# First layer's first pair of steps nested as well, the layer's pools opened after attention's are closed

## The chip, the cores and the metric

The kernel runs on one core of one Trainium2 chip. The metric is the device time of one execution in microseconds (us), taken as the median over runs. The engines are PE (TensorE, matrix products), DVE (VectorE), ACT (ScalarE), POOL (GpSimd) and SP (SyncE, which here only issues transfers). Each runs its own list of instructions in order and waits for the others on semaphores.

## The reference

Hashed attention, then a feed-forward layer. The results are float32; the two weight matrices come as float64.

```python
mask = q_bucket[:, :, :, None] == k_bucket[:, :, None, :]     # buckets: signs of q @ proj, k @ proj
scores = np.where(mask, q @ k.T / sqrt(D), -1e9)              # B, H, S, D = 4, 8, 768, 64
x = (softmax(scores) @ v)  -> (3072, 512)
h = x @ w_in                                                  # (512, 2048)
g = h * (1.0 / (1.0 + np.exp(-1.702 * h)))
out = g @ w_out                                               # (2048, 512)
```

## The kernel before

**Attention** (`attention`, to about 309 us) works through 16 pairs of heads. Its results stay transposed in `xT` (512 features by 3072 tokens). A pair's results are divided by their softmax sums at the end of the pair by `invert` and `norm` (L575 to L590, on DVE); for the last pair this runs when PE has already begun with the layer. The weights `w_in` arrive as float64 and are converted on the way (`convert`, L170 to L208: one transfer, six DVE steps, one square on ACT). The last two of their 16 chunks are left over (`LATE`) for the layer.

**The first product of the layer** (`feed_forward`) is `xT` by `w_in`, in three blocks of 1024 tokens (`sb`) and eight steps (`mt`) in a block, 24 in all. A step multiplies a 2 by 2 block matrix by another with seven products instead of eight (`product`, i = 1 to 7, L901), each two 128 by 128 weights against 512 tokens. For this it needs sums of quarters of the weights (`in_sums`, on POOL, L222 to L225, kept in `s_in` and, one of them, in `w_in_sb`) and of the tokens (`x_sums`, on DVE, L232 and L233, kept in `t_x`). After the products, ACT copies and DVE adds (L919) form four results u, v, c21, c22, ACT applies the activation (L916) and a transfer keeps them in `g_dram`. POOL then forms four sums of the four results for the second product (`g_outer`, L230 to L233) and SP stores these.

**Nested steps.** Steps are taken two at a time as a pair `t` where `t` lies in `NESTED`. Then three of the seven products (2, 4 and 3, for u, c21 and v) are split once more in the same way (`nested`): seven half-width products of 256 tokens (L971) take the place of four of 512. They need sums of their own: of the weights (`nest_w`, L222 to L225 on 128x128, kept in `nest`) and of the tokens (`nest_x`, L957 to L960, kept in rooms of `w_out_sb`). The other four products (1, 6, 5, 7) stay whole: `p1(0), p1(1), p6(0), p5(0), p6(1), p5(1), p7(0), p7(1)`. `plan(t, at, f)` puts a piece of work behind the `at`-th of these eight, and `play` issues it there; the numbers above 8 fall into the next pair. So the order on every engine is written out by hand by these plans.

**Buffers.** The four results of a pair lie in the pool `stage` for even `t` and in `twice` for odd `t`, so pair t + 2 writes where pair t was. Its first copy `u` (L1025) must wait until POOL has formed the sums that read pair t's `u` and SP has stored them. PSUM holds the accumulating banks: two of kind "a" (products 1, 6, 7), one of kind "b" (product 5), one "c" and the pool `inner` for the nested ones. Because "b" is one bank, `p5(1)` waits until DVE has added and ACT has copied `p5(0)` (L1035).

**Before the change** pair 0 isn't nested: its steps 0 and 1 run as `hidden(0, 0)` and `hidden(0, 1)`, each with seven whole products and a choice of eight banks. The first is built inside `attention`, after the pool that holds the exponentials is closed and while attention's other pools are still open: `attention` ends with `early.close()`, `whole(inverse)`, `norm(last)`, `next(ff)`. A one-element POOL copy, `behind_sums` (L1314), waits for the token sums ahead of `in_sums(1)` and `in_sums(2, 2)`. The pools `twice`, `nest`, `wop` (w_out and the rooms of `nest_x`) and `cv` open after `hidden(0, 0)`, and pairs 1 to 10 are nested.

**The second product** (L1240, from 585 us) multiplies what `g_dram` holds by `w_out`; its code isn't touched.

A part of the code behind a branch (`shifted_attention` and a second `feed_forward`) is not executed on these inputs.

Of the kernel before, what the change touches and what calls it, by code (L numbers as in the profile page):

```python
# [38 lines left out]
def kernel(  # L39
# [254 lines left out]
    def attention(ff):  # L294
# [4 lines left out]
        with actx:  # L299
# [463 lines left out]
            early.close()  # L763
            whole(inverse)
            norm(last)
            next(ff)


    def shifted_attention():
# [76 lines left out]
    def feed_forward(tag, late=()):  # L846
# [9 lines left out]
        with ExitStack() as fctx:  # L856
# [2 lines left out]
            late = list(late)  # L859

            outer = fctx.enter_context(tc.tile_pool(name=f"f0{tag}", bufs=1, space=PSUM, side="right"))
            small_ctx = fctx.enter_context(ExitStack())
            inner = None
            twice_ctx = fctx.enter_context(ExitStack())
            twice = None
            nest_ctx = fctx.enter_context(ExitStack())
            nest = None
            MT = FC // 2
            NESTED = range(1, MT + 3)
            sets = [small_ctx.enter_context(tc.tile_pool(name=f"f1{tag}", bufs=1, space=PSUM, side="right"))]  # L870
            todo, turn = {}, [-1]

            def outer_bank(name):
# [11 lines left out]
            def staged_pair(name, second):  # L885

                held[name] = (twice if second else stage).tile([P, 2 * XT], F32, tag=name, name=name)
                return held[name]

            def staged(name, n):  # L890

                if n in (0, 2 * NESTED.stop) and (name, n) not in made:
                    made[name, n] = staged_pair(name, n > 0)
                return held[name][:, n % 2 * XT : (n % 2 + 1) * XT]

            made = {}
# [115 lines left out]
            def pair_of_steps(t):  # L1012

                sb, m0 = divmod(2 * t, MT)
                tiles, a = {}, [None, None]

                def place(name, i):
                    if name not in tiles:
                        tiles[name] = staged_pair(name, t % 2 == 1)
                    return tiles[name][:, i * XT : (i + 1) * XT]  # L1020

                def p1(i):
                    a[i] = outer_bank("a")
                    product(a[i], sb, m0 + i, 1)
                    nc.scalar.copy(place("u", i), a[i])  # L1025

                def p6(i):
                    product(a[i], sb, m0 + i, 6, False)
                    nc.scalar.copy(place("v", i), a[i])

                def p5(i):
                    b = outer_bank("b")
                    product(b, sb, m0 + i, 5)
                    add(place("v", i), b, place("v", i))
                    nc.scalar.copy(place("c22", i), b)  # L1035

                def p7(i):
                    product(a[i], sb, m0 + i, 7, False)
                    add(place("c22", i), a[i], place("c22", i))
                    nc.scalar.copy(place("c21", i), a[i])  # L1040
                    if i:
                        emit(tiles["c22"])
                        keep(sb, m0, 3, tiles["c22"], nc.scalar)

                def done(at):
                    def f(x):
                        emit(x)
                        if at is not None:
                            keep(sb, m0, at, x, nc.scalar)
                    return f  # L1050

                def small(tag):
                    return lambda: inner.tile([P, XT], F32, tag=tag, name="small")

                for o, name, first, bank_of, at in ((2, "u", 3, lambda: outer_bank("c"), 0),
                                                    (3, "v", 4, small("y"), None), (4, "c21", 9, small("z"), 2)):
                    for i, f in zip((0, 2, 4, 6, 7), nested(o, sb, t, tiles, name, bank_of, done(at))):
                        plan(t, first + i, f, small=True)

                def g_part(i, j):  # L1060
                    x = [tiles[x].rearrange("p (m t) -> p m t", t=XT) for x in ("u", "v", "c21", "c22")]
                    if len(spare[t].shape) == 4 and i == 3:
                        x = [y.rearrange("p m (k t) -> p m k t", k=spare[t].shape[2]) for y in x]
                    g_outer(sb, m0, *x, x[0], x[3], spare[t])[i][j]()


                for i, at in enumerate((12, 13, 14, 17)):
                    for j in range(2):
                        plan(t, at + j, lambda i=i, j=j: g_part(i, j))
                order = (p1, 0), (p1, 1), (p6, 0), (p5, 0), (p6, 1), (p5, 1), (p7, 0), (p7, 1)  # L1070
                for at, (f, i) in enumerate(order, 1):
                    f(i)
                    play(8 * t + at)
# [222 lines left out]
            def conversions(cv, psum, chunks):  # L1296


                gens = [convert(cv, *x, nc.scalar if i else None, psum) for i, x in enumerate(chunks)]
                dma = next(gens[0])  # L1300
                if late:

                    behind_issue(dma, stored[2])
                yield
                for i, x in enumerate(gens):
                    for at in range(6):
                        next(x, None)
                        if at == 3 and i + 1 < len(gens):
                            next(gens[i + 1])
                        yield  # L1310


            behind_sums = stage.tile([1, 1], F32, name="behind_sums", bufs=1)
            nc.gpsimd.tensor_copy(behind_sums, t_x[0:1, 2, 0, 0:1])  # L1314
            for f in in_sums(1) + in_sums(2, 2):
                f()
            hidden(0, 0)
            yield
            twice = twice_ctx.enter_context(tc.tile_pool(name=f"tw{tag}", bufs=1, side="right"))
            nest = nest_ctx.enter_context(tc.tile_pool(name=f"ne{tag}", bufs=1, side="right"))  # L1320
            wop = fctx.enter_context(tc.tile_pool(name=f"wo{tag}", bufs=1))
# [27 lines left out]
            places += [[xT[:, k, XT * j : XT * (j + 1)] for k in (1, 0) for j in range(2)] + places[0][4:],  # L1349
                       [xT[:, k, XT * j : XT * (j + 1)] for k, j in ((2, 1), (0, 3), (1, 3), (1, 1), (0, 1), (2, 3))]]  # L1350
            places = [[x[:, j * TH : (j + 1) * TH] for x in y for j in range(2)] for y in places]
            more, w_sums = nest_x(0, places[0]), nest_w(1)
            x = todo.pop(1, [])
            hidden(0, 1, more[2] + w_sums[2] + more[3] + w_sums[3] + x[:4], x[4:])
            yield
            small_ctx.close()
            inner_ctx = fctx.enter_context(ExitStack())
            inner = inner_ctx.enter_context(tc.tile_pool(name=f"in{tag}", bufs=1, space=PSUM, side="right"))
            plan(1, 1, *more[4], *w_sums[4])
            for t in NESTED:  # L1360
                sb, at = divmod(t, MT // 2)
                if at == 0:
                    for i, f in enumerate(more[2] + more[3]):
                        plan(t, 1 + i // 2, f)
                    plan(t, 8, *(x[3] for x in x_sums))
# [169 lines left out]
```

## Time and profile before

| | |
|---|---|
| three runs | 847.32, 847.37, 848.08 us; median 847.37 |
| the profiled execution | 847.66 us |
| its span, first to last instruction | 845.9 us |
| granted TensorE clock | 0.997 |
| DVE busy | 674.9 us (80%) |
| ACT busy | 337.6 us (40%) |
| POOL busy | 382.3 us (45%) |
| moved by DMA | 144.92 MB |

How to read the profile: times are us from the start of the span unless ns is written. A row of the timeline gives start, duration, engine, source line, operation, output <- input, shapes, how many instructions were merged, and in brackets the idle time ahead of it with what ended it. A row of the chain gives start, duration, what. Each float32 matmul shows as two instructions, so a whole product (two weights) shows as x4 and a nested one as x2. Ends of matmuls are modelled, and merged rows of PE overlap the next by 0.16 us.

### The profile page before, as it was taken

How to read it: one execution, taken by the hardware profiler on the slowest of the kernel's cores; microseconds unless marked ns; L12 is line 12 of the kernel's file. 1: busy time of each engine (PE TensorE's matmuls, PEld its weight loads, DVE VectorE, ACT ScalarE, POOL GpSimd, SP SyncE). 2: the span in 40 equal slices, each digit the busy share in tenths (PEclk: the TensorE clock that was granted, in tenths of full speed). 3: DMA queues.
4: the chain of work that ended last, by engine and by line, in shares of the span. 5: the costliest groups of instructions: out<-in, count | busy, mean ns of one | idle time of the engine just before them, and what ended most of it. 6: DMA issues, size and time to landing. Idle time of an engine off the chain costs nothing.

```text
span 845.9 us, 14969 instructions
## 1 busy us (share of the span) xinstructions
PE 835.8 (99%) x5662; PEld 522.2 (62%) x5662; DVE 674.9 (80%) x1073; ACT 337.6 (40%) x550; POOL 382.3 (45%) x324
## 2 busy tenths in 40 slices
PE   8999999999999999999999999999999999999996
PEld 4444444444444444556666666656888888888885
DVE  5478888887888985786878678858999987797776
ACT  6766766766676634444444444443000000000000
POOL 4433443343334359999844686858865100000000
PEclk9999999999999999999999999999999999999998
DMA  9688666677674104446555546667844486467524
GB/s 142 121 156 172 152 137 142 139 153 148 152 160 100 50 2 174 149 139 235 205 195 200 221 174 224 221 226 249 303 182 165 177 236 256 155 194 249 199 100 101
DMA packets 165341, 144.92 MB, mean 171 GB/s; under 512 B 124112, under 2 KB 140112, under 8 KB 160272
## 3 DMA queue, kind: packets, MB, share of 16 engines
q1 hardware_dynamic: 154352, 110.54, 46.9%
q10 hardware_dynamic: 10912, 33.39, 11.8%
q8 instruction: 45, 0.74, 0.4%
q14 instruction: 32, 0.26, 0.1%
HBM read 79.69 MB, written 50.33 MB: 154 GB/s over the span
## 4 chain that ended last, share of the span: by engine, by line
PE 98%; DMA 1%; DVE 0%; SPq 0%; issue 0%; DVEq 0%
PE product L1240 30%; PE product L901 22%; PE s L547 15%; PE s L514 15%; PE small L971 7%; PE product L971 4%; PE s L496 2%; PE s L460 1%; PE s L569 1%; DMA pj<-in_proj_dram 1%; PE s L410 0%; DVE feat L411 0%; DVE own L405 0%; DVE y L1220 0%; SPq L385 0%
## 5 line engine op out<-in xcount | busy, mean ns | idle before, releaser
L484 ACT ACTIVATE e<-s 128x768 f32<-128x768 f32 x192 | 143.2, 811 | 48.5 <-PE s L514 43.9
L547 PE MATMUL s<-e,v 128*32 128x385 f32 x1536 | 130.9, 488 | 0.0
L525 POOL TENSOR_TENSOR t_x<-e 128x768 f32<-128x768 f32 x32 | 60.5, 1892 | 136.7 <-ACT e L484 131.8
L901 PE MATMUL product<-xT,w_in_sb 128*128 128x512 f32 x208 | 96.8, 592 | 0.0
L547 PEld LDWEIGHTS s<-e,v 128*32 128x32 f32 x1536 | 46.7, 109 | 79.3 <-issue 62.2
L901 PE MATMUL product<-t_x,s_in 128*128 128x512 f32 x192 | 89.7, 592 | 0.0
L514 PE MATMUL s<-s_in 32*128 32x384 f32 x912 | 87.8, 481 | 0.0
L525 POOL TENSOR_TENSOR t_x<-t_x,e 128x768 f32<-128x768 f32 x32 | 55.2, 1725 | 43.4 <-ACT e L484 42.0
L538 DVE TENSOR_TENSOR acc<-acc,e 128x768 f32<-128x768 f32 x63 | 70.1, 1112 | 2.3
L1276 ACT COPY wide<-product 128x256 f32<-128x256 f32 x20 | 7.4, 371 | 157.7 <-PE product L1240 116.2
L901 PEld LDWEIGHTS product<-xT,w_in_sb 128*128 128x128 f32 x208 | 39.4, 190 | 31.8 <-issue 28.9
L514 PEld LDWEIGHTS s<-s_in 32*128 32x128 f32 x912 | 43.9, 185 | 23.4 <-issue 2.2
L901 PEld LDWEIGHTS product<-t_x,s_in 128*128 128x128 f32 x192 | 36.4, 190 | 28.1 <-issue 25.6
L919 DVE TENSOR_TENSOR u<-product,u 128x256 f32<-128x256 f32 (+1 forms) x64 | 29.7, 478 | 23.5 <-PE product L971 21.2
L514 PE MATMUL s<-own 32*128 32x384 f32 x432 | 44.2, 482 | 0.0
L465 DVE TENSOR_SCALAR f<-s,above,weight 128x384 bf16<-128x384 f32 x15 | 10.2, 677 | 39.6 <-PE s L569 28.9
L230 POOL TENSOR_TENSOR u<-v,u 128x1024 f32<-128x1024 f32 (+1 forms) x12 | 26.2, 2184 | 20.8 <-ACT v L916 12.4
L919 DVE TENSOR_TENSOR c<-small,c 128x256 f32<-128x256 f32 (+1 forms) x60 | 26.8, 461 | 9.8 <-PE small L971 9.5
L535 DVE SCALAR_TENSOR_TENSOR acc<-t_x,e 128x768 f32<-128x768 f32 x31 | 29.3, 945 | 6.1 <-POOL t_x L525 3.5
L919 DVE TENSOR_TENSOR v<-small,v 128x256 f32<-128x256 f32 (+1 forms) x60 | 27.1, 465 | 8.4 <-PE small L971 5.8
L1035 ACT COPY c<-product 128x512 f32<-128x512 f32 x20 | 11.7, 586 | 52.2 <-DVE v L919 46.7
L1240 PE MATMUL product<-s_in,xT 128*128 128x256 f32 x136 | 31.3, 379 | 0.0
(302 smaller groups left out, 1808.0 us busy)
## 6 DMA issues: line engine op xcount, KB each, us to landing
raw_g<-g_dram SPq DMA_DIRECT2D x20, 1024.0 KB, 6.1
s_in<-g_dram SPq DMA_DIRECT2D x18, 1024.0 KB, 5.9
g_dram<-c ACTq DMA_DIRECT2D x20, 512.0 KB, 3.1
raw<-in_moe_w_out_dram ACTq DMA_DIRECT2D x16, 512.0 KB, 3.8
raw<-in_moe_w_in_dram ACTq DMA_DIRECT2D x15, 512.0 KB, 3.8
s_in<-own SPq DMA_DIRECT2D x36, 192.0 KB, 4.0
v<-in_v_dram SPq DMA_DIRECT2D x16, 384.0 KB, 4.2
g_dram<-u ACTq DMA_DIRECT2D x10, 512.0 KB, 2.9
```

What stands on the lines that cost most here:

```text
L230: return [lambda: eng.tensor_tensor(t1, b12, b11, op=Alu.subtract), lambda: eng.tensor_tensor(b12, b22, b12, op=Alu.subtract), lambda: eng ...
L484: nc.scalar.activation(es[c][:, kt, :, 0:HS], ps[:, :, 0:HS], Act.Exp, scale=1.0 / D**0.5)
L496: nc.tensor.matmul(ps[:, j, 0:HS], a[hs, keys], m[hs, cols], start=at == 0, stop=at == 1)
L514: nc.tensor.matmul(ps[i][:, j, 0:HS], a[r0 : r0 + 32, keys], m[r0 : r0 + 32, cols], start=at == 0, stop=at == 2)
L525: nc.gpsimd.tensor_tensor(low_sum, low_sum if i else e[:, 0], e[:, i + 1], op=Alu.add)
L535: nc.vector.scalar_tensor_tensor(acc, terms[0], T * TINY, terms[1], op0=Alu.add, op1=Alu.add)
L538: nc.vector.tensor_tensor(acc, acc, terms[i + 1], op=Alu.add)
L547: nc.tensor.matmul(av[D * j + d : D * j + d + 32, :], vt[:, j, row, d : d + 32], es[c][:, t, j, :], start=(t == 0), stop=(t == T - 1))
L901: nc.tensor.matmul(ps, wq[LEFT[i]][:, kc, :], xq[RIGHT[i]][:, kc, :], start=(start and kc == 0), stop=(kc == K2 - 1), skip_group_check=not ...
L919: nc.vector.tensor_tensor(dst, x, y, op=Alu.add)
L971: nc.tensor.matmul(x, wq[LEFT[i]], xq[RIGHT[i]], start=start, stop=True, skip_group_check=True)
L1240: nc.tensor.matmul(ps, wq[LEFT[i]][:, c, :], gq[RIGHT[i]][:, c, :], start=(onto is None and c == 0), stop=(c == F4 - 1), skip_group_check= ...
```

## The change

- `NESTED` begins at 0: pair 0 is nested like the others, and `hidden(0, 0)`, `hidden(0, 1)`, `behind_sums` and the small PSUM pool for them go.
- `next(ff)` at the end of `attention` goes: the layer's first pools open after all of attention's are closed.
- POOL's sums for pair 0 (`in_sums(1)`, and those of `nest_w(0)` and `nest_x(0)`) are put in the order in which its products use them; those of pair 1 and `in_sums(2, 2)` follow. `nest_w(0)` is no longer formed a second time at pair 3.
- In pair 0 the nested products stand later: u behind products 4, 6, 7, 9, 10, v behind 6, 7, 8, 10, 11 (otherwise 3, 5, 7, 9, 10 and 4, 6, 8, 10, 11).
- The transfer for the first late chunk of `w_in` is no longer put behind a store, and its conversion falls into pair 0.

```diff
@@ attention
             whole(inverse)
             norm(last)
-            next(ff)
@@ feed_forward
-            small_ctx = fctx.enter_context(ExitStack())
-            NESTED = range(1, MT + 3)
-            sets = [small_ctx.enter_context(tc.tile_pool(name=f"f1{tag}", bufs=1, space=PSUM, side="right"))]
+            NESTED = range(MT + 3)
+            sets = []
...
-                for o, name, first, bank_of, at in ((2, "u", 3, lambda: outer_bank("c"), 0),
-                                                    (3, "v", 4, small("y"), None), (4, "c21", 9, small("z"), 2)):
-                    for i, f in zip((0, 2, 4, 6, 7), nested(o, sb, t, tiles, name, bank_of, done(at))):
-                        plan(t, first + i, f, small=True)
+                for o, name, by, bank_of, at in ((2, "u", (3, 5, 7, 9, 10) if t else (4, 6, 7, 9, 10), lambda: outer_bank("c"), 0),
+                                                 (3, "v", (4, 6, 8, 10, 11) if t else (6, 7, 8, 10, 11), small("y"), None),
+                                                 (4, "c21", (9, 11, 13, 15, 16), small("z"), 2)):
+                    for i, f in zip(by, nested(o, sb, t, tiles, name, bank_of, done(at))):
+                        plan(t, i, f, small=True)
...
-                dma = next(gens[0])
-                if late:
-
-                    behind_issue(dma, stored[2])
+                next(gens[0])
...
-            behind_sums = stage.tile([1, 1], F32, name="behind_sums", bufs=1)
-            nc.gpsimd.tensor_copy(behind_sums, t_x[0:1, 2, 0, 0:1])
-            for f in in_sums(1) + in_sums(2, 2):
-                f()
-            hidden(0, 0)
-            yield
...
-            more, w_sums = nest_x(0, places[0]), nest_w(1)
-            x = todo.pop(1, [])
-            hidden(0, 1, more[2] + w_sums[2] + more[3] + w_sums[3] + x[:4], x[4:])
-            yield
-            small_ctx.close()
             inner_ctx = fctx.enter_context(ExitStack())
             inner = inner_ctx.enter_context(tc.tile_pool(name=f"in{tag}", bufs=1, space=PSUM, side="right"))
-            plan(1, 1, *more[4], *w_sums[4])
+
+            more, w_sums = nest_x(0, places[0]), nest_w(0)
+            for f in in_sums(1) + w_sums[2][:3] + more[2][:3]:
+                f()
+            plan(0, 2, *w_sums[3][:3], *more[3][:2], *w_sums[2][3:], *more[2][3:], *more[3][2:], *w_sums[3][3:])
+            plan(0, 7, *w_sums[4], *more[4])
             for t in NESTED:
                 sb, at = divmod(t, MT // 2)
-                if at == 0:
+                if at == 0 and t:
...
-                if t + 1 <= MT // 2:
-                    w_sums = nest_w((t + 1) % (MT // 2))
-                    if t + 1 < MT // 2:
-                        plan(t, 4 if t == 1 else 1, *in_sums(2 * t + 2, 2))
-                    plan(t, 6 if t == 1 else 3, *w_sums[2], *w_sums[4], *w_sums[3])
+                if t + 1 < MT // 2:
+                    w_sums = nest_w(t + 1)
+                    plan(t, (5, 4, 1)[t], *in_sums(2 * t + 2, 2))
+                    if t:
+                        plan(t, 6 if t == 1 else 3, *w_sums[2], *w_sums[4], *w_sums[3])
+                    else:
+                        plan(1, 1, *w_sums[2], *w_sums[3])
+                        plan(1, 5, *w_sums[4])
```

More of the change, by code (lines that the diff above doesn't have):

```diff
@@ L890, in staged @@
             def staged(name, n):
-                if n in (0, 2 * NESTED.stop) and (name, n) not in made:
-                    made[name, n] = staged_pair(name, n > 0)
+                if n == 2 * NESTED.stop and (name, n) not in made:
+                    made[name, n] = staged_pair(name, True)
                 return held[name][:, n % 2 * XT : (n % 2 + 1) * XT]
```

## The prediction

> **What bounds the kernel now.** I read the page first, for the engines and the chain that ended last, and then the table by stages for the first four pairs of steps.
>
> ```profile
> span 845.9 us, 14969 instructions
> PE 835.8 (99%) x5662; PEld 522.2 (62%) x5662; DVE 674.9 (80%) x1073; ACT 337.6 (40%) x550; POOL 382.3 (45%) x324
> ...
> PE 98%; DMA 1%; DVE 0%; SPq 0%; issue 0%; DVEq 0%
> ```
>
> ```profile
> 308.89:332.97 24.08, 24.08 (x58) 10.69 (x58) 15.98 (x24) 9.59 (x16) 20.83 (x23) 1.00 0.34 121
> 332.97:350.17 17.20, 17.20 (x50) 9.13 (x49) 13.06 (x22) 6.34 (x11) 16.42 (x24) 1.00 0.40 138
> 350.17:372.96 22.79, 22.79 (x76) 14.05 (x75) 18.58 (x35) 8.85 (x13) 21.69 (x34) 1.00 0.28 93
> ```
>
> The columns of the second view are length, busy time of PE, weight loads, DVE, ACT and POOL, then clock and DMA. PE is the chain, and in these stages (steps 0 and 1, pair 1, pair 2) it is busy for the whole length. So before the change no wait costs anything here, and the change can gain only by giving PE less to do. The same rows show what stands behind PE: POOL is busy for 21.69 of 22.79 us. PE is full, and POOL almost.
>
> **Less work for PE.** The durations of a product are those of the chain:
>
> ```profile
> 340.81 1.72 PE product L901 x4
> 342.53 0.86 PE product L971 x4
> ```
>
> A whole product (x4) takes 1.72 us; the second row holds two nested ones, 0.43 us each. Steps 0 and 1 are 14 whole products, 14 x 1.72 = 24.08, the length of the first stage. Nested, pair 0 is 8 whole and 21 nested ones: 13.76 + 9.03 = 22.79. The change takes **1.29 us** from PE, no more. The Trainium skill (Perfetto Trace Analysis, Matmuls) says that larger matmuls are more efficient than smaller ones; here half the width takes exactly half the time, so the measurement decides, and if the rule ate the whole gain the result would be 1.3 us higher.
>
> **The first wait: product 5 of step 1.** The start of the layer lies beside the end of attention on DVE:
>
> ```profile
> 311.62 1.56 DVE L233 TENSOR_TENSOR t_x<-xT,t_x 128x1024 f32<-128x1024 f32 x1
> 313.11 0.94 DVE L590 TENSOR_TENSOR xT<-xT,rs 128x768 f32<-128x768 f32 x1
> ...
> 318.15 1.29 DVE L590 TENSOR_TENSOR xT<-xT,rs 128x768 f32<-128x768 f32 x1
> ...
> 340.49 0.69 DVE L919 TENSOR_TENSOR v<-product,v 128x512 f32<-128x512 f32 x1
> ```
>
> ```profile
> 341.22 0.59 ACT L1035 COPY c<-product 128x512 f32<-128x512 f32 x1 [1.79 <-DVE v L919]
> ```
>
> DVE is at attention's sums without a pause until its last `norm` (L590) ends at 318.15 + 1.29 = 319.44. Before, `hidden` had eight banks and nothing on PE needed DVE until then. Now pair 0 has one bank "b": p5(1) must wait until DVE has added p5(0) (L919, 0.69) and ACT has copied it (L1035, 0.59), and the add is queued behind that `norm`. PE comes to p5(1) after p1, p1, p6, p5 (6.88), one nested product (0.43) and p6 (1.72): 308.89 + 9.03 = 317.9.
>
> When does the `norm` end? POOL and DVE hold each other up where both run sums out of SBUF:
>
> ```profile
> 310.52 1.59 POOL L225 TENSOR_TENSOR s_in<-w_in_sb,s_in 128x256 f32<-128x256 f32 x1
> 313.39 0.70 POOL L1314 COPY behind_sums<-t_x 1x1 f32<-1x1 f32 x1 [1.29 <-DVE t_x L233]
> ...
> 316.67 0.73 POOL L225 TENSOR_TENSOR s_in<-w_in_sb,s_in 128x256 f32<-128x256 f32 x1
> ...
> 318.71 1.87 POOL L223 TENSOR_TENSOR w_in_sb<-w_in_sb 128x512 f32<-128x512 f32 x1
> ```
>
> The same sum takes POOL 1.59 us beside DVE's L232 and L233 and 0.73 us beside a transpose; the last `norm` takes 1.29 us beside POOL's L223 and the one before it 0.94. After the change POOL is idle at the last `norm` (0.35 less), but the four sums of `in_sums(1)` move forward from behind `behind_sums` to 312.1, against L233, the earlier `norm` and L208. Bounds: 319.1, if they cost DVE nothing more than before, and 320.2, if DVE waits out one and a half of them besides (0.73 each). I take 319.6, nearest to the row of before. The Trainium skill (SBUF — State Buffer, Who interferes with whom) says that a DVE instruction with two SBUF inputs and a POOL instruction that reads SBUF exclude each other for the whole instruction; the rows agree in size, and by the full rule for two of DVE's sums I would put it at 319.8, 0.2 us more in the result.
>
> So p5(1) starts at 319.6 + 0.69 + 0.59 and about 0.1 for the two hand-overs, at 320.95: **PE waits 3.0 us** where it waited for nothing.
>
> **POOL starts late.** In the built program POOL's first sum for pair 0's nested weights (`w20`) waits for that same last `norm`, since `nest` now lies where attention's pools lay. The row of `behind_sums` shows such a release: DVE ended at 311.62 + 1.56 = 313.18, POOL began at 313.39. So POOL stands idle from about 315.2, when `in_sums(1)` is done, to 319.8, and everything for pairs 0 to 3 queues behind that. The durations, as distances between starts:
>
> ```profile
> 329.51 0.73 POOL L957 TENSOR_TENSOR w_out_sb<-xT 128x256 f32<-128x256 f32 x1
> ...
> 332.39 0.46 POOL L222 TENSOR_TENSOR w<-w_in_sb 128x128 f32<-128x128 f32 x1
> 332.93 0.45 POOL L223 TENSOR_TENSOR w_in_sb<-w_in_sb 128x128 f32<-128x128 f32 x1
> 333.34 0.46 POOL L224 TENSOR_TENSOR w<-w,w_in_sb 128x128 f32<-128x128 f32 x1
> ...
> 334.30 0.73 POOL L957 TENSOR_TENSOR w_out_sb<-xT 128x256 f32<-128x256 f32 x1
> ...
> 349.10 1.28 POOL L222 TENSOR_TENSOR s_in<-w_in_sb 128x512 f32<-128x512 f32 x1
> 354.28 0.46 POOL L222 TENSOR_TENSOR w<-w_in_sb 128x128 f32<-128x128 f32 x1
> 365.15 0.46 POOL L222 TENSOR_TENSOR w<-w_in_sb 128x128 f32<-128x128 f32 x1
> ```
>
> (The last three rows begin groups with others between.) Four `nest_x` sums take 332.39 - 329.51 = 2.88, four `nest_w` sums 1.91, `in_sums` of two steps 354.28 - 349.10 = 5.18. Nested product 6 of u needs the fifth POOL sum, 319.8 + 2.95 = 322.75; PE is there at 320.95 + 1.72 = 322.67. Each such meeting (u's, v's and then c21's product 6, whose sums stand behind `in_sums(2, 2)`) costs between 0 and 0.4; I take **0.6 us** in all. To this point PE is 3.0 + 0.6 - 1.29 = 2.3 us later than before.
>
> **The wait that decides: pair 3 takes over pair 1's buffers.**
>
> ```profile
> 370.49 2.36 POOL L230 TENSOR_TENSOR u<-v,u 128x1024 f32<-128x1024 f32 x1
> 372.93 2.37 POOL L231 TENSOR_TENSOR v<-c,v 128x1024 f32<-128x1024 f32 x1
> 375.37 2.36 POOL L232 TENSOR_TENSOR c<-c,u 128x1024 f32<-128x1024 f32 x1
> ...
> 380.14 0.46 POOL L222 TENSOR_TENSOR w<-w_in_sb 128x128 f32<-128x128 f32 x1
> ```
>
> ```profile
> 378.18 1.07 ACT L1025 COPY u<-product 128x512 f32<-128x512 f32 x2 [2.04 <-DMA g_dram<-u]
> ```
>
> ```profile
> 378.93 1.88 PE L901 MATMUL product<-t_x,s_in 128*128 128x512 f32 x4
> ```
>
> Pair 3's copy of u (ACT, two of 0.59 merged) waits until POOL's L232 has read pair 1's u and SP has stored it; it begins 2.81 us after L232. Pair 3's p6(0) overwrites the bank that it reads, and starts at 378.93; the first copy is done at 378.77. Before the change this fitted with 0.16 us to spare. Afterwards POOL's list from 319.8 to that L232 is: weights and tokens of u and v 2 x 1.91 + 2 x 2.88 = 9.58; `in_sums(2, 2)` 5.18; c21's 1.91 + 2.88; pair 1's u and v weights 3.82; L230 of pair 0 2.44; `in_sums(4, 2)` 5.18; c21's weights 1.91; L231, L232 of pair 0 4.88; pair 2's weights 5.73; L233 2.44; `in_sums(6, 2)` 5.18; pair 3's weights 370.49 - 365.15 = 5.34; L230, L231 of pair 1 4.88. Sum 61.35. A sum that needs the one right before it starts 0.54 after it, otherwise 0.41 (332.39, 332.93, 333.34); the new order has about five fewer such neighbours, so 60.75. L232 begins at 319.8 + 60.75 = 380.55 instead of 375.37, **5.2 us later**; less the spare time (0.16, of which 0.05 is the hand-over) PE's p6(0) is 5.1 us later than before, at 384.0. By its own work and the first waits it would be there at 381.2, so this wait takes in the 2.3 us and is not added to it. Bounds of the list: 60.0, if every sum runs without the 0.13, and 61.9.
>
> **Nothing later gives back or adds.** Before, POOL formed `nest_w(0)` again at 380.14, 5.7 us of work, which is gone now; so POOL is 0.5 us ahead for pair 2's sums while PE is 5.1 later. The first late chunk of `w_in` starts to load at the `norm` and has some 5 us until DVE comes to it; pair 0's stores go by ACT (0.33 each) beside idle time of ACT. If such cover failed, it would cost under 1 us and end inside the 2.8 us that PE waits at pair 3.
>
> The sum: 847.66 (profiled execution; 845.9 of span and 1.76 around it) + 5.1 = 852.8. The median of the runs is 0.29 below the profiled one, so **852.5**.
>
> **Rivals.** (a) *Only the first waits count* (8%): POOL gets through its list 2.8 us faster than its rows say, and +2.3 remains: 849.7. Against it: from 329.51 to 375.37 POOL's rows of before follow each other without idle time. (b) *Not slower* (5%): the last `norm` doesn't hold the layer, PE keeps its 1.29 us, 846.1. Place: the release of POOL's `w20` and of DVE's first add. It decides only if both come by 316.5 for p5(1), and POOL's list by 313.3 for pair 3 (375.37 - 1.3 - 60.75); DVE's rows stand against it, for it only that the two engines would disturb each other less. That nested products don't do what they say (no gain on PE) is 1.3 above any of these, but the rows of pairs 1 and 2 speak against it. (c) *More than one takeover waits* (8%): stores of v and c22 of pair 1, which also come after POOL's later sums, hold pair 3's copies long enough to stop p5(1) too, another 2 to 3 us, 855. Against: ACT needs that copy only some 9 us after p6(0). The forecast has the other 79%.
>
> **Numbers.** For the forecast: `norm` 319.1 to 320.2 and list 60.0 to 61.9 give +3.9 to +6.8, as ends that won't all meet; 850.9 to 854.2 takes most of it, and leaves (a), (b) and (c) out. About 0.2% (1.7 us) is what a measurement of this kernel can tell from no change. Even the ideal, 1.29 us, is within that: faster 1%, same 5%, slower 94%.
>
> **What would show it.** In the profile after: PE's rows with about 3 us of nothing before the second p5 near 318 to 321; POOL idle from about 315 to 320, released by DVE's L590; POOL's second L230 group (pair 1's) about 5 us later than 370.49; a gap of about 2.8 us on PE before pair 3's p6(0), with ACT's u copy released by POOL or the store; and no gap from there on. I am wrong if POOL's first nested sum starts before the last `norm`, or if the gap at pair 3 isn't there.

## The result and the profile after

After: **851.83 us** median of six runs (851.45 to 853.37); before, beside it: 847.35 us (six runs, 846.68 to 848.08). The ratio is 1.0057 (95% interval 1.0044 to 1.0070), some 4.5 us slower. The profiled execution of after took 853.05 us; that of before 847.66.

In after the lines have shifted by two: products are L899 (whole) and L969 (nested), DVE's adds L917, ACT's copies L1023, L1033 and L1038. The page of after, its first lines:

```profile
span 851.2 us, 14995 instructions
...
PE 838.1 (98%) x5680; PEld 528.0 (62%) x5680; DVE 678.8 (80%) x1089; ACT 338.1 (40%) x548; POOL 382.3 (45%) x319
```

Span and busy time alone say little: PE stands idle some 3 us more, and its busy time grew too, although the change takes work away (there are 18 more matmul instructions, 5680 for 5662, but more of them are half as wide). The table by stages of after says more (columns as in the prediction: length, busy time of PE, weight loads, DVE, ACT, POOL, clock, DMA). Its stretches are cut where PE stops and starts:

```profile
308.36:317.81 9.45, 9.44 (x23) 3.91 (x22) 9.16 (x14) 2.39 (x5) 7.91 (x8) 1.00 0.01 3
317.81:320.25 2.44, 0.00 (x1) 0.00 (x0) 2.07 (x4) 0.64 (x2) 0.97 (x3) 1.00 0.18 22
...
380.73:382.87 2.14, 0.17 (x2) 0.01 (x1) 1.91 (x4) 0.64 (x2) 2.06 (x2) 1.00 0.92 364
382.87:388.10 5.23, 5.23 (x12) 3.34 (x13) 0.79 (x3) 3.30 (x5) 1.96 (x2) 0.67 0.78 301
388.10:590.67 202.57, 202.57 (x644) 121.98 (x643) 150.68 (x272) 84.38 (x120) 134.85 (x76) 1.00 0.58 208
```

Two stretches have almost no work on PE, 2.44 and 2.14 us (the 0.17 in the second row is the overlap of merged rows); behind the second PE ran 5.23 us at a mean granted clock of 0.67; from there to the second product nothing is idle. PE's timeline names who ended the two gaps:

```profile
315.83 1.98 PE L899 MATMUL product<-t_x,s_in 128*128 128x512 f32 x4
320.25 1.98 PE L899 MATMUL product<-t_x,s_in 128*128 128x512 f32 x4 [2.44 <-ACT c L1033]
...
382.87 2.56 PE L899 MATMUL product<-t_x,s_in 128*128 128x512 f32 x4 [1.97 <-ACT u L1023]
385.22 1.06 PE L969 MATMUL small<-xT,w 128*128 128x256 f32 x2
```

The first gap is p5(1) of pair 0, the second p6(0) of pair 3. The last row shows the slow clock in the work itself: this nested product (x2) is followed by the next after 0.85 us instead of 0.43. The engines that PE waited for, DVE, ACT and POOL of after in turn:

```profile
318.02 0.96 DVE L590 TENSOR_TENSOR xT<-xT,rs 128x768 f32<-128x768 f32 x1
318.90 0.68 DVE L917 TENSOR_TENSOR v<-product,v 128x512 f32<-128x512 f32 x1
```

```profile
319.61 0.59 ACT L1033 COPY c<-product 128x512 f32<-128x512 f32 x1 [5.32 <-DVE v L917]
...
382.23 1.07 ACT L1023 COPY u<-product 128x512 f32<-128x512 f32 x2 [4.28 <-POOL c L232]
```

```profile
315.85 0.72 POOL L225 TENSOR_TENSOR s_in<-w_in_sb,s_in 128x256 f32<-128x256 f32 x1
319.20 0.45 POOL L222 TENSOR_TENSOR w<-w_in_sb 128x128 f32<-128x128 f32 x1 [2.62 <-DVE xT L590]
...
379.84 2.35 POOL L232 TENSOR_TENSOR c<-c,u 128x1024 f32<-128x1024 f32 x1
```

One chain runs through the first gap (last `norm`, DVE's add, ACT's copy, PE) and one from the same `norm` to the second: POOL idle for 2.62 us, its list of 60.64 us (319.20 to 379.84), L232, ACT's copy, PE. That POOL waits for this `norm` because `nest` lies where attention's pools lay is argued: its first sum reads only `w_in_sb`, which the `norm` doesn't touch, and the profile shows no addresses.

**Where the time went.** The layer's start differs between profiled runs (308.89 before, 308.36 after, up to 309.0 in kernels that don't touch what lies ahead of it), so I count from it. The table of before, for two distances:

```profile
308.89:378.93 70.04, 70.04 (x199) 37.53 (x199) 51.51 (x87) 28.13 (x45) 64.75 (x81) 1.00 0.38 130
378.93:584.94 206.01, 206.01 (x656) 124.26 (x655) 155.22 (x277) 87.55 (x124) 141.22 (x89) 1.00 0.60 217
```

Pair 3's p6(0) comes 70.04 us after the layer's start in before and 382.87 - 308.36 = 74.51 in after: +4.47. That is -1.29 of work, +2.87 at p5(1) (due at 315.23 + 0.43 + 1.72 = 317.38), +2.14 in the second gap, and the 0.75 that is left, in small waits. From there to the second product it is 206.01 before and 590.67 - 382.87 = 207.80 after: +1.79, the slow clock. So the profiled execution pays 6.26. The median's 4.5 has the size of the sum without that last item; that the runs near the median didn't pay it is argued under 1, not shown, since only one execution of a kernel is profiled.

### The profile page after: what moved, and what is told of

Its sections match the earlier page's. It is cut to its first block, busy times and chain, and to the rows that moved or that the text cites. A ratio compares the mean times of both kernels' runs of the same rounds, so it can differ in the third digit from the quotient of the medians.

```text
span 851.2 us, 14995 instructions
## 1 busy us (share of the span) xinstructions
PE 838.1 (98%) x5680; PEld 528.0 (62%) x5680; DVE 678.8 (80%) x1089; ACT 338.1 (40%) x548; POOL 382.3 (45%) x319
## 4 chain that ended last, share of the span: by engine, by line
PE 94%; DVE 2%; POOL 1%; issue 1%; ACT 0%; DMA 0%; DVEq 0%; POOLq 0%
PE product L1240 30%; PE product L899 19%; PE s L514 15%; PE s L547 15%; PE small L969 8%; PE product L969 4%; PE s L496 2%; PE s L460 1%; PE s L569 1%; DMA raw<-in_moe_w_out_dram 0%; POOL v L231 0%; POOL c L232 0%; ACT e L484 0%; DVE rs L584 0%; POOL above L339 0%
## 5 line engine op out<-in xcount | busy, mean ns | idle before, releaser
L899 PE MATMUL product<-t_x,s_in 128*128 128x512 f32 x192 | 90.8, 597 | 4.4 <-ACT c L1033 2.4
L899 PE MATMUL product<-xT,w_in_sb 128*128 128x512 f32 x200 | 93.5, 592 | 0.0
L899 PEld LDWEIGHTS product<-t_x,s_in 128*128 128x128 f32 x192 | 36.2, 190 | 32.6 <-issue 24.4
L899 PEld LDWEIGHTS product<-xT,w_in_sb 128*128 128x128 f32 x200 | 37.9, 190 | 28.2 <-issue 25.4
L917 DVE TENSOR_TENSOR u<-product,u 128x256 f32<-128x256 f32 (+1 forms) x68 | 31.1, 471 | 25.4 <-PE product L969 23.6
L917 DVE TENSOR_TENSOR v<-small,v 128x256 f32<-128x256 f32 x66 | 29.8, 465 | 12.5 <-PE small L969 9.8
L917 DVE TENSOR_TENSOR c<-small,c 128x256 f32<-128x256 f32 x66 | 29.6, 462 | 11.4 <-PE small L969 11.1
L1033 ACT COPY c<-product 128x512 f32<-128x512 f32 x22 | 12.9, 586 | 59.5 <-DVE v L917 53.7
L230 POOL TENSOR_TENSOR u<-v,u 128x1024 f32<-128x1024 f32 x11 | 26.0, 2363 | 23.1 <-ACT v L914 13.1
L231 POOL TENSOR_TENSOR v<-c,v 128x1024 f32<-128x1024 f32 (+1 forms) x13 | 31.3, 2409 | 0.8
```

Of the source, the lines that this page charges most:

```text
L230: return [lambda: eng.tensor_tensor(t1, b12, b11, op=Alu.subtract), lambda: eng.tensor_tensor(b12, b22, b12, op=Alu.subtract), lambda: eng ...
L231: lambda: eng.tensor_tensor(b12, b22, b12, op=Alu.subtract),
L899: nc.tensor.matmul(ps, wq[LEFT[i]][:, kc, :], xq[RIGHT[i]][:, kc, :], start=(start and kc == 0), stop=(kc == K2 - 1), skip_group_check=not ...
L917: nc.vector.tensor_tensor(dst, x, y, op=Alu.add)
```

## The experiments

Theory: POOL's late start at attention's last `norm` sets the time through the takeover of pair 1's buffers by pair 3, and the first wait lies inside that. Rivals: the first wait alone counts; or the takeover has slack, and something else holds pair 3. The runs, each beside runs of before on the same chip, all with the two distances of their profiled execution (layer's start to pair 3's p6(0), and to the second product; before: 70.04 and 276.05, after: 74.51 and 282.31):

| | median us (range) | before, same chip | ratio (95%) | to p6(0) | to 2nd product |
|---|---|---|---|---|---|
| 1 | 850.01 (849.04-850.62) | 847.33 | 1.0029 (1.0018-1.0039) | 72.37 | 278.37 |
| 2 | 851.48 (851.30-851.76) | 847.33 | 1.0046 (1.0032-1.0060) | 74.50 | 280.61 |
| 3 | 850.01 (849.25-850.71) | 847.33 | 1.0030 (1.0018-1.0042) | 72.36 | 278.37 |
| 4 | 852.23 (851.89-852.37) | 847.33 | 1.0055 (1.0042-1.0069) | 75.03 | 281.15 |
| 5 | 852.42 (851.63-854.45) | 847.62 | 1.0059 (1.0046-1.0073) | 75.20 | 281.21 |
| 6 | 855.20 (854.58-856.60) | 847.62 | 1.0092 (1.0076-1.0107) | 75.81 | 283.71 |
| 7 | 849.44 (849.10-849.77) | 847.62 | 1.0017 (1.0008-1.0026) | 72.35 | 278.35 |
| 8 | 848.74 (848.51-849.66) | 847.62 | 1.0013 (1.0004-1.0022) | 71.21 | 277.22 |
| 9 | 848.35 (847.89-850.02) | 847.79 | 1.0005 (0.9996-1.0014) | 71.36 | 277.37 |
| 10 | 848.15 (847.62-848.57) | 847.79 | 1.0003 (0.9994-1.0012) | 70.24 | 276.25 |
| 11 | 847.53 (847.10-848.65) | 847.79 | 1.0000 (0.9991-1.0009) | 70.46 | 276.47 |
| 12 | 851.96 (851.37-852.33) | 847.79 | 1.0048 (1.0034-1.0062) | 74.40 | 280.51 |

**1. Pair 3's weight sums behind pair 1's L230 to L232** (twelve sums, 5.3 us, out of the list ahead of the takeover).

```diff
-plan(t, 6 if t == 1 else 3, *w_sums[2], *w_sums[4], *w_sums[3])
+plan(t, 6 if t == 1 else 7, *w_sums[2], *w_sums[4], *w_sums[3])
```

> The changed kernel with one edit: POOL's twelve sums for pair 3's nested weights (5.3 us) stand behind pair 1's L230 to L232 instead of ahead of them. Theory (the takeover of pair 1's buffers by pair 3 sets the time, and the slow clock after it is its consequence): pair 1's L232 begins at about 374.5 instead of 379.84, PE has no gap at pair 3 (2.1 us back) and its clock stays at 1.00 there (1.8 us back): 847.9. Rival A (the first wait, at the second product 5, is what counts): no change, 851.8. Rival B (the slow clock of pair 3 has another cause, such as the heavy transfers there): only the gap goes, 849.7.

POOL's L232 in this kernel, then its table by stages:

```profile
374.45 2.36 POOL L232 TENSOR_TENSOR c<-c,u 128x1024 f32<-128x1024 f32 x1
```

```profile
317.77:320.21 2.44, 0.01 (x1) 0.00 (x1) 2.06 (x4) 0.64 (x2) 0.97 (x3) 1.00 0.15 20
320.21:380.68 60.47, 60.45 (x195) 36.72 (x196) 45.99 (x86) 26.21 (x38) 58.20 (x74) 1.00 0.45 163
380.68:586.68 206.00, 206.00 (x655) 124.25 (x654) 153.49 (x277) 87.18 (x123) 138.68 (x81) 1.00 0.59 213
```

L232 is 5.39 us earlier than in after, and the second gap and the slow clock behind it are gone: p6(0) at 72.37, then 206.00 as in before. The first gap stays. So rival A is out, and in this trace rival B as well, for the clock stayed whole at pair 3. The median of 850.01 missed the expected 847.9 all the same, and lies at rival B's number. The profiled span fell by 4.0 us, the median only by 1.8; the 847.9 took 1.8 us of slow clock off a median that need not have held them. That fits a slow clock that most runs of after had where it cost nothing (12 shows such a place; four of after's six runs have a mean clock of 0.996), and that some runs of this kernel had behind the first gap, where nothing takes it in now: its three runs of 849.0 to 849.4 show a mean clock of 0.998, the five of 849.8 to 850.6 one of 0.996 to 0.997. A mean of 0.997 decides nothing by itself: before's profiled run has it too, from 4.8 us at half rate behind its last product. The six runs of the third kernel split without that doubt: 849.25 to 849.75 at 0.998 and 0.999, 850.26 to 850.71 at 0.995 and 0.996. In the second kernel, where pair 3 still waits for POOL, a run at 0.996 took 851.31 and three at 0.998 took 851.30 to 851.67. For the single runs of after it stays argued. What is left, +2.33 at p6(0), is the size the prediction gave the first waits.

**2. p7(0) ahead of p5(1) in pair 0**, to give DVE time at the first wait, and **3. both edits.**

```diff
+if t == 0:
+    order = (p1, 0), (p1, 1), (p6, 0), (p5, 0), (p6, 1), (p7, 0), (p5, 1), (p7, 1)
```

> The changed kernel with one edit: in pair 0 PE issues p7(0) ahead of p5(1), so that it has 1.7 us of work before the product that waits for DVE. Theory (pair 3's takeover sets the time): the first wait shrinks from 2.9 to about 1.2 us, PE comes to pair 3 1.7 us earlier and waits 3.9 there instead of 2.1; the time stays, 851.8, or rises by up to 1 if a longer gap makes the slow clock longer. Rival A (the first wait counts): 850.1.

> Both edits of the two kernels before: pair 3's weights behind pair 1's sums, and p7(0) ahead of p5(1). Theory: with the takeover out of the way the first wait counts in full, so its 1.7 us come back now: 847.9 - 1.7 = 846.2, which is 1.1 below the kernel before the change. Rival A: 850.1. Rival B: 848.0.

PE's timeline of the second kernel:

```profile
322.58 1.21 PE L969 MATMUL product<-w_out_sb,w 128*128 128x256 f32 x2 [2.61 <-POOL w_out_sb L956]
```

The first wait didn't shrink, it moved: u's second nested product stands behind the same slot and needs POOL's fifth sum. Yet p6(0) of pair 3 came at 74.50, as in after, though the nested product's row also shows the clock halved behind the gap. With POOL's list as in after, pair 3 starts when POOL lets it, whatever PE lost earlier: what PE lost to the slow clock came out of the gap at pair 3, which shrank to 0.69. The median agrees with the expected 851.8 but can't tell the rivals apart, since the first wait kept its size. In the third kernel p6(0) came at 72.36, as in the first; its expected 846.2 was a miss, because the wait was still there.

**4. Work for POOL in its idle time**: two of the four sums of `in_sums(2, 2)` ahead of `w20`.

```diff
-for f in in_sums(1) + w_sums[2][:3] + more[2][:3]:
+ahead = in_sums(2, 2)
+for f in in_sums(1) + ahead[:2] + w_sums[2][:3] + more[2][:3]:
...
-plan(t, (5, 4, 1)[t], *in_sums(2 * t + 2, 2))
+plan(t, (5, 4, 1)[t], *(in_sums(2 * t + 2, 2) if t else ahead[2:]))
```

> The changed kernel with one edit: two of the four sums of in_sums(2, 2) (2.6 us) move ahead of w20, into the time in which POOL stands idle until the last norm. Theory (POOL's late start pushes its list, and so the takeover): the list after the norm is 2.6 us shorter, the norm ends up to 0.4 later because POOL now disturbs it, so pair 1's L232 is 2.2 to 2.6 earlier, the gap of 2.1 at pair 3 closes and the clock stays: 847.9 to 848.4. Rival A: 851.8 to 852.2. Rival C (POOL's list isn't what is late, but the transfer of pair 1's u): gap and time stay, 851.8.

POOL's rows with idle time in this kernel:

```profile
320.23 0.46 POOL L222 TENSOR_TENSOR w<-w_in_sb 128x128 f32<-128x128 f32 x1 [1.03 <-DVE xT L590]
340.94 2.37 POOL L230 TENSOR_TENSOR u<-v,u 128x1024 f32<-128x1024 f32 x1 [0.22 <-ACT v L914]
345.16 1.27 POOL L222 TENSOR_TENSOR s_in<-w_in_sb 128x512 f32<-128x512 f32 x1 [1.85 <-DVE w_in_sb L208]
```

No gain where 847.9 to 848.4 was expected; the median lies at the number of rivals A and C. The rows say why without speaking against the theory: the `norm` came 1.0 us later beside POOL's sums, and 1.85 + 0.22 us of the lead were lost again waiting for DVE's conversion of the last chunk of `w_in` and for ACT. L232 of pair 1 came 72.0 us after the layer's start instead of 71.5, and p6(0) 0.5 later with it. Against rival C: ACT's copy of u begins 2.38 to 2.41 us after the start of L232 in all six kernels in which POOL is late for pair 3 (after, 2, 4, 5, 6, 12), right at L232's end.

**5. and 12. The second gap filled** with eight, then five, matmuls on PE whose results nothing uses.

```diff
 def p6(i):
+    if t == 3 and i == 0:
+        x = outer_bank("b")
+        for _ in range(8):      # 12: range(5)
+            nc.tensor.matmul(x, idle[:, 0:P], idle, start=True, stop=True)
```

> Kernel after, with eight extra 512-wide bf16 matmuls on PE just before pair 3's p6(0). They write a bank that nothing reads, so they compute nothing. They lie in the gap in which PE waits for ACT's copy of u. Theory: the wait itself ends when POOL and ACT say so, so p6(0) starts where it did; but PE is busy until then, the slow clock that followed this gap in the profile of after (about 1.8 us) does not come, and no run reaches the 853.05 and 853.37 that two runs of after took: median 851.3 to 851.8, profiled run about 851.5. Rival: the slow clock has nothing to do with the gap, the runs spread as those of after do, up to 853.4.

> The fifth experiment with five of the extra matmuls instead of eight (1.08 us instead of 1.73), so that they end before ACT's copy also when PE comes to the gap late. They compute nothing that is used. Theory: pair 3's p6(0) starts 74.5 us after the layer's start as in after, and with PE idle for 1.1 us there instead of 2.1 no slow clock follows: 851.3 to 851.8, no run above 852.3. Rival: as after, 851.4 to 853.4.

The table by stages of the twelfth:

```profile
317.90:320.34 2.44, 0.00 (x1) 0.00 (x0) 2.07 (x4) 0.64 (x2) 0.97 (x3) 0.92 0.18 20
320.34:323.64 3.30, 3.30 (x5) 1.51 (x6) 0.00 (x0) 0.44 (x1) 3.14 (x6) 0.54 0.41 149
...
382.86:392.00 9.14, 9.14 (x31) 5.62 (x31) 7.02 (x13) 4.74 (x7) 6.49 (x3) 1.00 0.79 280
```

In the profiled executions of both the clock fell at the *first* gap (a mean of 0.54 for 3.3 us of work here) and stayed whole behind the filled one. In the twelfth, p6(0) came at 74.40 all the same: what the slow clock cost in pair 0 was taken in by the wait at pair 3. The fifth was a flawed test: PE came late from the slow clock in pair 0, and eight matmuls (1.73 us) outlasted the wait and cost 0.7 us of their own. Its median of 852.42 missed the expected 851.3 to 851.8, and one of its five runs took 854.45 at a mean clock of 0.999, so a long run doesn't need a slow clock; what made that one long stays open. The twelfth's median of 851.96 lies 0.16 above its expected range and its highest run at its edge; no run reached 853. With five runs that agrees with the slow clock as cause of after's two runs above 853, and doesn't prove it.

**6. The takeover alone, in the kernel before**: twelve extra sums ahead of pair 1's L230, nothing of the change.

```diff
+x = nest.tile([P, P], F32, name="extra")
+plan(2, 3, *[lambda: nc.gpsimd.tensor_tensor(x, xT[:, 0, 0:P], xT[:, 1, 0:P], op=Alu.add)] * 12)
```

> Kernel before, with twelve extra sums of 128x128 on POOL (0.41 each, about 5.0 us) ahead of pair 1's L230; their results aren't read. Nothing else of the change is in it: no nested pair 0, no wait at attention's end. Theory: the takeover of pair 1's buffers by pair 3 decides, with 0.1 to 0.2 us to spare, so PE waits about 4.9 us before pair 3's p6(0), and ends 4.8 to 6.6 us later (the upper end with a slow clock behind the gap): 852.2 to 854.0. Rival: POOL has slack, or pair 3 waits for something else, and the time stays within 1 us of 847.4.

POOL's timeline, PE's, and the table by stages of this kernel:

```profile
370.51 6.35 POOL L1378 TENSOR_TENSOR extra<-xT 128x128 f32<-128x128 f32 x12
...
381.69 2.34 POOL L232 TENSOR_TENSOR c<-c,u 128x1024 f32<-128x1024 f32 x1
```

```profile
384.71 3.77 PE L901 MATMUL product<-t_x,s_in 128*128 128x512 f32 x4 [5.61 <-ACT u L1025]
```

```profile
379.10:381.75 2.65, 0.00 (x1) 0.00 (x0) 2.04 (x4) 0.00 (x0) 2.49 (x3) 0.95 0.49 198
381.75:384.71 2.96, 0.00 (x1) 0.01 (x1) 0.00 (x0) 0.64 (x2) 2.88 (x2) 0.50 0.44 177
384.71:388.30 3.59, 3.59 (x5) 1.52 (x6) 0.00 (x0) 1.39 (x2) 3.43 (x5) 0.50 0.75 296
388.30:394.00 5.70, 5.70 (x20) 3.53 (x19) 4.38 (x9) 2.77 (x4) 5.39 (x10) 1.00 0.39 111
```

The sums took 6.35 us, not 5.0 (0.53 each: all write one tile, and a sum behind a neighbour that it depends on starts 0.54 later, as the prediction's rows had it). L232 is 6.32 later than in before, p6(0) 5.77 later, and the second product another 1.89: 7.66 in all, and the medians differ by 7.6. The expected range was low by the 1.3 us that I had mispriced; the mechanism is shown: p6(0) starts 3.02 us after L232, as in after (3.03), and a late POOL alone, with PE's work untouched, makes the gap at pair 3 and the slow clock behind it. The slack rival is out.

**7. Pair 0 in another order**: the first experiment's edit, the order of the second, and the nested products where their sums are ready.

```diff
-(3, 5, 7, 9, 10) if t else (4, 6, 7, 9, 10)      # u
+(3, 5, 7, 9, 10) if t else (4, 7, 8, 9, 10)
-(4, 6, 8, 10, 11) if t else (6, 7, 8, 10, 11)    # v
+(4, 6, 8, 10, 11) if t else (5, 8, 9, 10, 11)
```

> Kernel after with pair 3's weight sums behind pair 1's L230 to L232, as in the first experiment, and pair 0 in another order: p7(0) ahead of p5(1), and the nested products of u behind slots 4, 7, 8, 9, 10 and of v behind 5, 8, 9, 10, 11, so that nothing that needs POOL's first five sums stands ahead of p5(1). PE reaches p5(1) 10.3 + 0.9 = 11.2 us after the layer's start, at 319.5 on the profiled run's clock, against the copy's end at 320.2. Theory: the first wait falls from 2.9 to about 0.7 us, with no gap long enough for a slow clock, and PE's 1.29 us saved pay for it and the small waits: 847.0 to 847.6. Rival: a wait again takes the first one's place (POOL's sums for product 6, 2 us or more) and the time stays near the 850.0 of the first experiment.

PE's waits in this kernel:

```profile
320.64 1.98 PE L899 MATMUL product<-t_x,s_in 128*128 128x512 f32 x4 [0.29 <-ACT c L1033]
...
325.88 0.67 PE L969 MATMUL product<-w_out_sb,w_in_sb 128*128 128x256 f32 x2 [0.49 <-DVE u L917]
...
337.54 0.70 PE L969 MATMUL small<-w_out_sb,w 128*128 128x256 f32 x2 [1.53 <-POOL w_out_sb L956]
```

The first wait is gone (0.29), and the time is 849.44, not 847.0 to 847.6: a miss. p6(0) stands at 72.35, to 0.02 us where it stood in the first experiment. A wait has taken the first one's place: c21's second nested product (337.54) needs POOL's L956, and 337.54 - 308.75 = 28.79 us after the layer's start it comes as early as POOL allows. In the first experiment that product stood at 28.81. So "the first wait" of 2.9 us was never worth 2.9: POOL's late start was to be paid at c21's sums anyway. The runs of this kernel lie within 0.7 us (849.10 to 849.77); no gap in it reaches 2 us.

**8. The last `norm` earlier**: as 7, with the conversion step between the last two norms moved into DVE's idle time near 303.

```diff
 if n == last:
     inverse[n - 1] = invert(n - 1)
     next(inverse[n - 1])
-    step(n, 2)
+    step(n, 3)
```

> The seventh experiment's kernel with one more edit: the last step (L208, 1.21 us of DVE) of the conversion of attention's last chunk of w_in is issued where DVE stands idle for 1.21 us near 303, instead of between the last two norms. Theory: the last norm, DVE's first add and POOL's release come up to 1.2 us earlier, so no first wait is left and PE keeps most of its 1.29 us: 845.9 to 846.6, faster than both kernels. Rival: attention is held up by as much (its sums on DVE come later), and nothing is gained: 847.0 to 847.6 as expected of the seventh.

DVE's timeline of this kernel:

```profile
303.03 2.07 DVE L208 SCALAR_TENSOR_TENSOR w_in_sb<-raw,w_in_sb 128x512 f32<-128x512 f32 x1
305.02 0.94 DVE L535 SCALAR_TENSOR_TENSOR acc<-e 128x768 f32<-128x768 f32 x1
```

POOL's first sum came 9.70 us after the layer's start instead of 10.84, and p6(0) 1.14 earlier than in 7: PE follows POOL one for one. Only 0.7 of that reached the medians. The step took 2.07 us beside a POOL sum (1.21 in after), and DVE's softmax sums began late: at 305.02, where after, whose DVE stood 0.07 us earlier at L201, began them at 304.14. From DVE's L201 (near 302) to the layer's first product it takes 7.41 us in 8 and in 10, and 6.79 to 6.81 in before, after, 1, 7, 9 and 11: attention ends 0.6 us later, as the rival said. 845.9 to 846.6 was a miss.

**9. c21's sums first in POOL's list**, on 7; **10.** the same on 8, with v's nested products ahead of u's; **11.** as 10, but without the eighth's edit, and with the conversion step behind the last `norm`.

```diff
-plan(0, 7, *w_sums[4], *more[4])
+ahead = in_sums(2, 2)
+plan(0, 7, *w_sums[4][:3], *more[4][:2], ahead[3], *w_sums[4][3:], *more[4][2:])
...
-plan(t, (5, 4, 1)[t], *in_sums(2 * t + 2, 2))
+plan(t, (5, 4, 1)[t], *(in_sums(2 * t + 2, 2) if t else ahead[:3]))
```

```diff
 norm(last - 1)
-step(last)
 inverse = invert(last)
 ...
 norm(last)
+step(last)      # 11 only
```

> The seventh experiment's kernel, with POOL's list changed at one place: the five sums that c21's second nested product needs come ahead of the fourth sum (1.27 us) of in_sums(2, 2) and of c21's fourth weight sum (0.41). In the seventh and in the first experiment PE stood at c21's second nested product until POOL's L956 let it go, 28.8 us after the layer's start in both, whatever had been waited for before; pair 3's p6(0) followed 72.35 us after the layer's start in both. Theory: POOL's late start at attention's last norm is what the layer still waits for, at c21's sums. With these 1.7 us earlier that wait (1.7 us) goes, pair 3's p6(0) starts 70.6 to 71.0 us after the layer's start, and the time falls from 849.4 to 847.6 to 848.1. Rival: the 28.8 us come from something else (DVE's adds, the bank) and the time stays at 849.1 to 849.8.

> The eighth experiment's kernel with the same change of POOL's list, and with v's nested products ahead of u's where both stand behind the same product of pair 0, so that u's third waits less for DVE. Theory: of the 1.35 and 0.87 us that PE lost at c21's and u's products there, 1.35 and some 0.5 go: 846.6 to 847.2, level with before or 0.1% under it. Rival: the moved conversion step delays attention by what it gives the layer, and the time is that of the ninth experiment or more.

> As the tenth, but the conversion step (L208) stands behind attention's last norm instead of ahead of it, and nothing in attention is moved forward. Theory: the last norm and with it POOL's first sum come about 1.2 us earlier after the layer's start than in the ninth (9.6 instead of 10.8 us), DVE's first add about 0.5 earlier; PE waits for at most 0.5 us in pair 0 and keeps most of its 1.29 us: 846.3 to 847.0. Rival: POOL's sums, no longer held apart from DVE, give the 1.2 us back, and the time is that of the ninth.

PE's rows of the ninth, then POOL's first nested sum in the eleventh:

```profile
336.03 0.59 PE L969 MATMUL small<-w_out_sb,w 128*128 128x256 f32 x2
...
357.47 1.98 PE L899 MATMUL product<-t_x,s_in 128*128 128x512 f32 x4 [0.63 <-ACT u L1023]
```

```profile
318.31 0.69 POOL L222 TENSOR_TENSOR w<-w_in_sb 128x128 f32<-128x128 f32 x1 [1.94 <-PE small L969]
```

In the ninth c21's product runs without a wait, 27.0 us after the layer's start, and p6(0) comes 1.0 earlier: the cause found in 7 is right. It isn't the expected 1.7, and 848.35 lies 0.25 above the expected range, because the next meeting takes 0.9 (from start to start of the products, 0.8 ahead of p6(0) and 0.1 in it): p6(0) of *pair 2* waits for ACT's copy, which waits for POOL to have read *pair 0's* buffers. The tenth reaches its second product 276.25 us after the layer's start, only 0.2 more than before, but attention ended 0.6 late, as told under 8, and 848.15 missed the expected 846.6 to 847.2: the rival was right that the moved step gives back most of what it brings. The eleventh has POOL's first sum 9.69 us after the layer's start (10.84 in 7 and 9) and leaves attention alone. Its row names PE as releaser; the last `norm` ended at 318.09 there, 0.22 ahead of the sum as in after (318.98 and 319.20), so the row can't tell the two apart. The moved L208 wasn't the releaser, for it ran until 318.69. The median: 847.53, level with before, though 0.5 above what was expected. Its second product still comes 276.47 after the layer's start, 1.7 more than 276.05 - 1.29: PE's starts lie apart by more than the matmuls' 1.72 and 0.43: 0.8 at v's second product (POOL), 0.6 at pair 2's takeover, 0.3 at p5(1). No version was faster than before.

## Why the prediction was right

- **PE saves 1.29 us**: agrees. In the eleventh kernel p6(0) of pair 3 stands 70.46 us after the layer's start; less the 1.7 us of waits read off PE's rows that is 68.76, and 70.04 - 1.29 = 68.75. Pair 2 of after, nested and without a wait, takes 22.79 us (351.91 to 374.70), as forecast for such a pair. That nested products at half width are less efficient isn't seen.
- **First wait 3.0**: 2.87. The `norm` ended 10.62 us after the layer's start, predicted 10.71; before it the sums of `in_sums(1)` and DVE's held each other up as argued (the earlier `norm` took 1.48 us instead of 0.94, POOL's sum beside L233 and that `norm` 1.71), and POOL's first nested sum was released by that `norm` (10.84 after the start; predicted 10.91).
- **POOL's list 60.75**: 60.64.
- **Gap before pair 3's p6(0)**: there, by the predicted chain, but 2.14 us, not 2.8. The mis-sized term is the step from L232 to ACT's copy: I took 2.81 us from before, where the store of pair 1's u ended the wait (DMA); in after the copy began 2.39 after L232, right at its end, and the trace names POOL. That is 0.42 of the difference; `norm` and list came 0.18 earlier than forecast. So +4.47 at p6(0) instead of +5.1, and a median of 851.83 instead of 852.5.
- **The takeover takes in the first waits**: shown by 2 and 12 (PE lost more in pair 0 to the slow clock, and p6(0) stayed at 74.4 to 74.5), by 4 (p6(0) moved by the 0.5 that L232 moved) and by 1 (+2.33 without the takeover, predicted +2.3).
- **Small waits 0.6**: 0.75. But "each such meeting costs between 0 and 0.4" holds only behind a first wait; without it c21's meeting alone costs 1.7 (7). That was not seen beforehand. Rival (a)'s +2.3 is what 1 measured once the takeover was out of the way (+2.33), but not because of the first wait: 7 took that wait away, and p6(0) stayed where 1 had it.
- **No gap from there on**: right for gaps. The slow clock behind the second gap, 1.79 us in the profiled run, was not foreseen. That the range held the profiled 853.05 as well is luck: its width was worked out for other terms. Rival (c) is out: no second takeover stops PE behind pair 3's p6(0).
- Rival (b), not slower, was out by the place it named: POOL's release would have had to come much earlier. Even with 1.15 us of that and a better order (11) the change only breaks even.

## What to carry to other kernels

Where PE is full, look for the engine that is second-fullest and lists its work in order: a late start there is passed on for tens of microseconds, to the first reuse of a buffer that has no slack, and shortening any earlier wait buys nothing until that one is gone. Opening a pool later can tie its first writer to the last user of whatever lay there before, however unrelated (here POOL stood idle for 2.62 us; that the place in memory was the reason is argued). And before an edit moves a wait, list the next two meetings of the same two engines; here three stood in a row (p5(1), c21's sums, the takeovers), each hidden by the one ahead.

## What the runs showed of the hardware

PE's granted clock fell to half at gaps of 2.1 to 2.6 us in some profiled executions and not in others: at the gap of 2.14 us in after but not at its 2.44, at 2.44 in the twelfth experiment but not in the first. The traces show what decides. Within each of the 14 profiled executions the times at which the granted clock changes lie whole multiples of 3.41 us apart. Cut on that grid, after reads:

```profile
315.87:319.28 3.41, 1.94 (x4) 0.63 (x4) 3.27 (x8) 0.00 (x0) 0.79 (x2) 1.00 0.00 0
319.28:322.70 3.42, 2.45 (x7) 1.19 (x8) 0.99 (x3) 1.07 (x2) 3.26 (x6) 1.00 0.49 153
...
380.72:384.14 3.42, 1.45 (x4) 0.68 (x4) 2.04 (x4) 1.91 (x3) 3.34 (x2) 1.00 0.91 362
384.14:387.55 3.41, 3.41 (x8) 2.19 (x7) 0.42 (x1) 1.48 (x3) 0.50 (x1) 0.50 0.77 296
387.55:390.96 3.41, 3.41 (x12) 1.99 (x11) 2.95 (x6) 0.88 (x3) 2.97 (x2) 1.00 0.09 32
```

The gap of 2.44 us falls on two pieces of the grid, 1.47 and 0.97 us of idle PE, and the clock stays whole. The gap of 2.14 us falls on one piece, 1.97 us of idle PE in it, and the whole next piece runs at half rate. In the layer's first product the clock fell behind every piece with 1.97 us or more without PE (after 1.97, twelfth 2.03, fifth 2.23, sixth 2.41, second 2.61, fourth 2.89) and behind none with 1.80 or less (third 1.80, after 1.47, first 1.32). In the sixth, with its gap of 5.61, two pieces in a row had too little work, and the clock was down for 6.83 us, from 2.4 us into the gap to 3.6 us after work had begun again. So where a gap falls on the grid decides whether it is paid for, and runs of one kernel need not agree in it. One slow piece cost 1.79 us of PE where no later wait took that in. The Trainium skill (TensorE: Matmul & The Clock Gate, Part 1: The HAM clock gate) describes a free-running window of about 3.4 us and half rate after an idle one; the traces agree in the window's length, but here 1.97 us without PE in a window were enough.
